# A gated mix of two attentions: the maximum of two key tiles as b + relu(a - b), with the key differences formed once, early

## The chip, the cores and the metric

The kernel runs on one core of one Trainium2 chip. A core has five engines with instruction queues of their own: TensorE (PE, matrix products; PEld is its weight load), VectorE (DVE), ScalarE (ACT), GpSimd (POOL) and SyncE (SP, which issues transfers). Products land in PSUM, eight banks of 128 partitions by 512 fp32 numbers; everything else lies in SBUF. The metric is the device time of one execution in microseconds (us); the median of three runs of the kernel before is 1503.92 us (1503.39 to 1504.63).

## The reference

```
x = A_x                                            # 1 x 2048 x 512
g = sigmoid((x * gate_w).sum(-1))
# branch A: 32 heads of 16, each query sees 8 keys at distances 0, 2, ... 14
qkv = x @ wqkv;  logits = q . k[idx] * 16**-0.5;  attn = softmax(logits)
a = (attn . v[idx]) @ wo_a
# branch B: 32 query heads of 16, one key head and one value head for all of them
q = x @ wq;  k = x @ wk;  v = x @ wv
scores = einsum("bhqd,bkd->bhqk", q, k) * 16**-0.5
b = (softmax(scores) . v) @ wo_b
out = g * a + (1 - g) * b
```

Branch B is the large part: 32 heads x 2048 queries x 2048 keys. Its weights are drawn eight times larger than those of branch A, so the scores are large and each row's maximum must be taken off before the exponential.

## The kernel before, in words

**Units and query buffers.** Branch B is cut into 32 units of four heads by 512 queries. The queries of a unit lie in a buffer `qst` (128 partitions by 2 by 512): two heads in partitions 0 to 63, two in 64 to 127, the fp32 numbers split in parts so that the fast product type keeps their digits. There are nine buffers (`NB`); unit u uses buffer u % 9. `stack(u)` fills one by four transfers on SP's queue from a DRAM scratch tensor `qd`. The keys `kst` lie in SBUF once, in the same split form, in both partition halves.

**Two passes over the scores.** The first pass needs only the maximum over all keys of each query. A unit has 64 *maximum tiles*: 128 queries by 512 keys, one product of 62 partitions each (`max_mm`). The result is reduced along the keys into `mx`. Three ways are used: a *pair* of tiles in a bank pair `pm` (`m2`), reduced by one DVE instruction (L334); a *single* tile in the bank `ps` (`m1`) or `po`, reduced by one DVE instruction (L346); and, in part of the kernel, two key tiles at once by *differences*. When a unit's 64 tiles are done, `shift_a` to `shift_d` write the negated maxima, split in two, into two spare partitions of each half of the unit's query buffer, by eight small transfers.

The second pass goes by *steps*: a step is one unit and one block of 128 keys, 16 steps per unit, 512 in all. In a step PE makes the scores again, now keys by queries and with the maximum taken off by the two extra partitions (L452, two products into each of two bank pairs `pe0`, `pe1`); ACT takes the exponential of each bank pair (L454); PE multiplies the exponentials with the values into `po` (L463, `weighted`). In between, the step takes up maximum tiles of later units: mostly one pair, and a single where `singles` allows one. `singles` spreads what is left over the steps that are left, so it decides how many steps have a single.

**The maximum by differences, before the change.** For two key tiles a and b the kernel forms, once, the half sums and half differences of the *keys*: `half_keys` multiplies `kst` by a selection matrix `sel` with entries 0.5 and -0.5 (L362), `half_parts` splits the results into `kcd`. Because a score is linear in its key, a product with the half difference gives (a - b)/2 and one with the half sum gives (a + b)/2. `fill_diff` makes the first in bank `pd0` or `pd1` (L384) and ACT writes its absolute value to SBUF (L394, `dd`). `fill_sum` makes the second in `ps` or `po` (L384), and one DVE instruction adds the two and takes the maximum (L404): (a + b)/2 + |a - b|/2 = max(a, b). So two maximum tiles cost two products, one ACT and one DVE instruction.

**The stages.** *Start*: loads, keys, the first two query blocks (L187, L824). *Query part*: the other 14 query projections, "lumps" of 12 products per array half (L1001, into four banks `pf`). *Branch A part*: 64 lumps that project branch A's queries, keys and values (L1001 too, 384 or 402 columns). *Steps*: the 512 steps, with three *output phases* among them (`out_phase`, L707) that project finished blocks. POOL computes the attention of branch A beside all this. In the query part and the branch A part, the two 64-partition halves of the array run as two streams, and maximum tiles are put between the products of the lumps. In the query part before, these are pairs and singles; `half_keys` and the differences begin with the branch A part, since `kcd`, `dd` and the two banks `pd` take memory that the query part uses for raw weights and for `pm`.

**What sets the order.** The schedule is manual: a planner in the kernel's Python keeps one clock for PE, ACT and DVE (`clk`), a time at which each bank comes free (`free`) and when a buffer is filled (`stacked`), and writes instructions engine by engine in that order when the program is built. On the chip nothing is reordered; an engine whose operand isn't ready waits. Three of the planner's rules matter here. `fillable` allows a maximum tile only for a unit whose query buffer is filled. `singles` is described above. And where a unit must soon begin its steps and its maxima aren't done (`short > 0 and steps < 2`), `pause` puts maximum tiles in a row, into `pe0`, `pe1` and `pm`, and no exponential goes on beside them.

Of the kernel before, what the change touches and what calls it, by code (L numbers as in the profile page):

```python
# [13 lines left out]
P = 128  # L14
# [34 lines left out]
def gated_mix_kernel(ctx, tc, xt, wa, wk, wq, wo_a, wo_b, out):  # L49
# [16 lines left out]
    qst = [cp.tile([P, 2, 512], F32R, name=f"qst{k}") for k in range(NB)]  # L66

# [31 lines left out]
    wqr = p0.tile([P, C, C, P], F32, name="wqr")  # L99
# [14 lines left out]
    def load_wq(cc):  # L114
        nc.scalar.dma_start(wqr[:, cc], wq[:, cc])

    def split_wq(cc):
        cs = slice(cc * P, (cc + 1) * P)
        split(wqh[:, :, cs], wql[:, :, cs], wqr[:, cc])
# [56 lines left out]
    for x in range(2):  # L176
        to = sel[:, x].rearrange("p (b h z) -> p b h z", b=2, h=2)
        nc.vector.tensor_scalar(to[:, :, 0].rearrange("p b (d s) -> p b d s", s=2), whole_k.unsqueeze(3).to_broadcast([P, 2, DH, 2]), 0.5 - x, 0.0, op0=ALU.mult, op1=ALU.add)
        nc.vector.tensor_scalar(to[:, :, 1].rearrange("p b (s d) -> p b s d", s=2), whole_k.unsqueeze(2).to_broadcast([P, 2, 2, DH]), 0.5 - x, 0.0, op0=ALU.mult, op1=ALU.add)
# [90 lines left out]

    def stack(u):
        qb, hg = divmod(u, NHG)
        for b in range(2):
# [3 lines left out]
            dst = qst[u % NB].rearrange("p c n -> p (c n)").bitcast(F32)  # L277
# [10 lines left out]
    free = {"m2": 0.0, "m1": 0.0, "e0": 0.0, "e1": 0.0, "po": 0.0}  # L288
    tasks, shifted, pm = [], set(), []
# [20 lines left out]
    def max_mm(dst, v, pr, t, kc, odd):  # L310
        b = 64 * odd
        nc.tensor.matmul(dst, qst[v % NB][b:b + 62, pr, t * P:(t + 1) * P], kst[b:b + 62, kc * 512:(kc + 1) * 512], start=True, stop=True)  # L312
# [4 lines left out]
    def filled(v, n):  # L317
        left[v] -= n
        if not left[v]:
# [7 lines left out]
            tasks.append((after("dve", 0, 0.66) + (2.0 if kcd and not pe else 0.1), shift_a, (v, mt)))  # L327
# [24 lines left out]
    kcd, dd, formed, ended = [], [], set(), set()  # L352
    pend, todo, ready_d, read_d = [[], []], [[], []], [0.0, 0.0], [0.0, 0.0]

    wanted = []

    def half_keys(g):

        clk["pe"] = max(clk["pe"], free["d0"], free["d1"])
        for x in range(2):  # L360
            for y in range(2):
                nc.tensor.matmul(ds[x], sel[:, x * y], kst[:, (2 * g + y) * 512:(2 * g + y + 1) * 512], start=(y == 0), stop=(y == 1))  # L362
        clk["pe"] += 1.2
        up = ups[0]
        free["d0"] = free["d1"] = clk["pe"] + 4.0
        tasks.append((clk["pe"] + 1.0, half_parts, (g, up)))

    def half_parts(g, up):
        for x in range(2):
            got = nc.scalar.activation(kcd[0][:, g, x], ds[x], AF.Identity, scale=mk[:, 0:1])  # L370
            at = after("act", clk["pe"], 0.65)
            mark(got, at, up)
        for x in range(2):
            parts = kcd[0][:, g, x]
            nc.vector.scalar_tensor_tensor(parts, ds[x], mk[:, 1:2], parts.bitcast(F32), op0=ALU.mult, op1=ALU.add)
            free[f"d{x}"] = after("dve", at + 0.1, 0.7) + 0.1
        formed.add(g)
# [4 lines left out]
    def half_mm(dst, v, pr, t, kc, x, odd):  # L382
        b = 64 * odd
        nc.tensor.matmul(dst, qst[v % NB][b:b + 62, pr, t * P:(t + 1) * P], kcd[0][b:b + 62, kc // 2, x, :], start=True, stop=True)  # L384

    def fill_diff(b):
# [6 lines left out]
        half_mm(ds[b], v, pr, t, kc, 1, b)  # L393
# [874 lines left out]
```

## Time and profile before

| what | value |
|---|---|
| median of three runs | 1503.92 us |
| the profiled execution | 1504.23 us, of which 1502.4 us span |
| granted clock of PE over the span | 0.998 |
| PE, PEld, DVE, ACT, POOL busy | 99%, 48%, 82%, 81%, 63% |
| 0 to 27 us | start |
| 27 to 78 us | query part |
| 78 to 274 us | branch A part |
| 274 to 1479 us | the 512 steps and three output phases |
| 1479 to 1502 us | the last rows of the output |

Times in the profile count from the span's start. A "x8" in a row is the number of instructions merged in it; what stands in brackets is how long the engine had been idle before, and what ended that. PE's busy share is high all through, but an instruction's time there runs from its start to its modelled end, and neighbours overlap: the distance between starts tells more than the busy share. The profiled execution has 1.8 us outside the span.

### The profile page before, as it was taken

The page shows a single profiled execution, that of the slowest core. Times are in us where ns is not written, and L with a number is a line of the kernel's source. Part 1 is how long each engine was busy: PE and PEld are TensorE (multiplying, and loading weights), DVE is VectorE, ACT ScalarE, POOL GpSimd, SP SyncE. Part 2 cuts the span into 40 slices and gives each one's busy share as a digit, 9 for nine tenths or more (in the row PEclk, how much of TensorE's full clock was granted, in tenths as well). Part 3 has the DMA queues.
Part 4 walks back from the last instruction along what each step waited for, and adds up shares of the span by engine and source line. Part 5 has one row for each costly group of instructions (what it writes and reads, how often), then busy time and mean ns, then how long its engine had stood idle before and what let it go on. Part 6 is the DMA issues. An engine that isn't in the chain of part 4 may idle for free.

```text
span 1502.4 us, 28913 instructions
## 1 busy us (share of the span) xinstructions
PE 1483.1 (99%) x10947; PEld 726.8 (48%) x10947; DVE 1234.6 (82%) x1777; ACT 1219.0 (81%) x1527; POOL 948.3 (63%) x1671
## 2 busy tenths in 40 slices
PE   8999999999999999999999999999999999999998
PEld 5899999433333333333333463333335533733335
DVE  6977888788888888888888888888888888888821
ACT  4357988799999999999999759999996688399884
POOL 7423988888888988888888988889812211410100
PEclk9999999999999999999999999999999999999999
DMA  6744242121221120120211112112000000000000
GB/s 219 197 125 141 83 153 94 62 77 41 62 73 41 48 77 23 65 76 12 76 41 51 59 40 70 41 40 70 13 12 8 22 2 2 30 2 1 1 2 29
DMA packets 43964, 85.63 MB, mean 57 GB/s; under 512 B 9568, under 2 KB 26016, under 8 KB 39728
## 3 DMA queue, kind: packets, MB, share of 16 engines
q1 hardware_dynamic: 36128, 43.99, 9.7%
q0 software_dynamic: 6688, 37.96, 7.6%
q8 instruction: 86, 1.41, 0.4%
q10 hardware_dynamic: 1008, 1.84, 0.4%
q14 instruction: 54, 0.44, 0.1%
HBM read 57.97 MB, written 25.25 MB: 55 GB/s over the span
## 4 chain that ended last, share of the span: by engine, by line
PE 95%; DVE 2%; ACT 1%; DMA 1%; issue 0%; POOL 0%; SPq 0%; ACTq 0%; DVEq 0%; POOLq 0%
PE po L463 33%; PE pe L452 26%; PE pf L1001 11%; PE pm L312 9%; PE ps L312 5%; PE pe L707 4%; PE pd L384 2%; DVE mx L334 1%; PE po L384 1%; PE ps L384 1%; PE pe L1199 1%; PE pf L187 1%; DMA xraw<-xt 1%; ACT pexp L454 0%; PE po L312 0%
## 5 line engine op out<-in xcount | busy, mean ns | idle before, releaser
L454 ACT ACTIVATE pexp<-pe 128x1024 f32<-128x1024 f32 x1024 | 992.4, 1023 | 103.4 <-PE pe L452 99.0
L334 DVE TENSOR_REDUCE mx<-pm 128x2 f32<-128x1024 f32 x537 | 655.7, 1221 | 149.9 <-PE pm L312 142.0
L452 PE MATMUL pe<-qst,kst 64*128 64x512 f32 x2048 | 573.5, 456 | 2.9 <-DVE mx L334 1.8
L463 PE MATMUL po<-pexp,vst 128*32 128x512 f32 x4096 | 547.0, 606 | 0.6 <-DVE tt L477 0.4
L452 PEld LDWEIGHTS pe<-qst,kst 64*128 64x128 f32 x2048 | 235.3, 184 | 441.9 <-ACT pexp L454 434.2
L346 DVE TENSOR_REDUCE mx<-ps 128x1 f32<-128x512 f32 x536 | 364.7, 680 | 5.3 <-PE ps L312 3.0
L312 PE MATMUL pm<-kst,qst 62*128 62x512 f32 x1083 | 230.8, 406 | 2.5 <-DVE mx L334 2.0
L312 PE MATMUL ps<-kst,qst 62*128 62x512 f32 x536 | 226.1, 422 | 0.6 <-DVE mx L346 0.6
L525 POOL TENSOR_TENSOR pr<-aext 128x256 f32<-128x256 f32 x256 | 182.3, 740 | 4.9 <-PE pf L1001 4.7
L585 POOL TENSOR_TENSOR oa<-oa,av 128x256 f32<-128x256 f32 x224 | 164.4, 734 | 15.8
L463 PEld LDWEIGHTS po<-pexp,vst 128*32 128x32 f32 x4096 | 80.6, 108 | 181.5 <-issue 169.4
L582 POOL TENSOR_TENSOR av<-aext,lg 128x256 f32<-128x256 f32 x224 | 139.6, 623 | 13.5
L489 POOL TENSOR_TENSOR rl<-rl,gate_t 128x16 f32<-128x16 f32 x31 | 6.9, 221 | 213.0 <-DVE rl L483 212.9
L312 PEld LDWEIGHTS ps<-kst,qst 62*128 62x128 f32 x536 | 98.5, 184 | 84.4 <-DVE mx L346 79.6
L394 ACT ACTIVATE dd<-pd 128x512 f32<-128x512 f32 x186 | 109.8, 601 | 26.0 <-DVE mx L404 15.0
L1001 PE MATMUL pf<-wah,xh 64*128 64x384 f32 (+1 forms) x496 | 124.7, 338 | 0.0
L1001 PE MATMUL pf<-wah,xl 64*128 64x384 f32 (+1 forms) x496 | 122.4, 338 | 0.0
L1001 PE MATMUL pf<-wal,xh 64*128 64x384 f32 (+1 forms) x496 | 121.3, 337 | 0.0
L312 PEld LDWEIGHTS pm<-kst,qst 62*128 62x128 f32 x1083 | 106.2, 187 | 18.3 <-DVE mx L334 11.4
L531 POOL TENSOR_TENSOR tr<-pr 128x512 f32<-128x512 f32 x64 | 81.7, 1277 | 4.2
L531 POOL TENSOR_TENSOR tr<-tr 128x256 f32<-128x256 f32 (+1 forms) x128 | 72.5, 566 | 9.0
L404 DVE CUSTOM_DVE_ANT_0 dd<-po,dd 128x512 f32<-128x512 f32 x93 | 64.2, 690 | 16.4 <-PE po L384 10.6
(198 smaller groups left out, 1688.6 us busy)
## 6 DMA issues: line engine op xcount, KB each, us to landing
aext<-ad POOLq DMA_DIRECT2D x32, 1056.0 KB, 5.4
ad<-stage SPq DMA_DIRECT2D x32, 384.0 KB
qst<-qd SPq DMA_DIRECT2D x64, 128.0 KB
xraw<-xt SPq DMA_DIRECT2D x16, 256.0 KB
qd<-qhi SPq DMA_DIRECT2D x16, 256.0 KB
qd<-qlo SPq DMA_DIRECT2D x16, 256.0 KB
qst<-qd SPq DMA_DIRECT2D x64, 64.0 KB
qst<-ml SPq DMA_DIRECT2D x224, 2.0 KB
```

The source lines that it names most:

```text
L312: nc.tensor.matmul(dst, qst[v % NB][b:b + 62, pr, t * P:(t + 1) * P], kst[b:b + 62, kc * 512:(kc + 1) * 512], start=True, stop=True)
L334: got = nc.vector.tensor_reduce(m[:, :, pr, t, kc], dst, AX.X, ALU.max)
L346: got = nc.vector.tensor_reduce(m[:, odd, pr, t, kc:kc + 1], dst, AX.X, ALU.max)
L394: got = nc.scalar.activation(dd[0][:, b], ds[b], AF.Abs)
L452: nc.tensor.matmul(bank[:, odd, :], kst[b:b + 64, kt * P:(kt + 1) * P], qst[u % NB][b:b + 64, pr, :], start=True, stop=True)
L454: got = nc.scalar.activation(e, bank, AF.Exp, scale=SCALE)
L463: nc.tensor.matmul(po[32 * i:32 * i + 32, :], vst[:, kt, :], pexp[s, i // 2][:, i % 2, :], start=(kt == 0), stop=(kt == NJ - 1))
L525: nc.gpsimd.tensor_mul(pr[:, k], q, e[:, o:o + NH, AC:2 * AC])
L531: nc.gpsimd.tensor_add(nx, cur[:, :, 0:n], cur[:, :, n:2 * n])
L582: nc.gpsimd.tensor_mul(av, e[:, o:o + NH, 2 * AC:].rearrange("p j (h d) -> p j h d", d=DH), lg[:, w].unsqueeze(3).to_broadcast([P, NH, AG, ...
L585: nc.gpsimd.tensor_add(ao, ao, av)
L1001: inst = nc.tensor.matmul(home(x)[0][:, :n], l[h], r[h], start=(i == 0 and b == 0), stop=(i == 3 * C - 1 and b == 1))
```

## The change

**The maximum.** For two key tiles a and b, max(a, b) = b + relu(a - b). The key differences a - b are still formed by a product with `sel`, now with entries 1 and -1; b is the key tile itself, as it lies in `kst`. So `fill_diff` multiplies with `kd` and ACT writes relu in place of the absolute value; `fill_sum` multiplies with `kst` by `max_mm`. The half sums aren't formed: `half_keys` is one call of four products in place of two calls of eight in all, `half_parts` splits two results in place of four.

**Memory and time.** `kd` and `dd` take the SBUF memory of the raw query weights (four blocks of `wq`, loaded and split in the start), which are from the constant pool now. The two banks `pd0`, `pd1` exist from the start, in place of the bank pair `pm`, which comes only with the steps. So `half_keys` runs at the beginning of the query part, and differences are used there already. The first pair before the query part is gone, and the maximum tiles are taken unit by unit from the start.

**Query buffers.** The buffers of the output phases (`own`, `turned`) are no longer tiles of their own: they lie in query buffers 7 and 8, which after units 7 and 8 hold no queries. Units from 9 on go round through seven buffers (`place`). `stack` is therefore called two units later from the sixteenth unit on, and the last rows use other buffers.

```diff
+    wq01 = cp.tile([P, 2, 512], F32, name="wq01", tag="kd", bufs=1)
+    dd = cp.tile([P, 2, 512], F32, name="dd")
...
-    pp2 = tc.alloc_tile_pool(name="pairs", bufs=1, space=PSUM)
-    m2 = pp2.tile([P, 2, 512], F32, name="pm")
-    ds = []
+    pp2, m2 = None, None
+    pools = [tc.alloc_tile_pool(name="parts", bufs=1, space=PSUM)]
+    ds = [pools[0].tile([P, 512], F32, name=f"pd{k}") for k in range(2)]
...
+    def place(v):
+        return v if v < NB else (v - NB) % (NB - 2)
...
-    slots = [(v, pr, t, kc) for kc in range(2) for v in range(2) for pr in range(2) for t in range(4)]
-    slots += [(v, pr, t, kc) for v in range(2) for pr in range(2) for t in range(4) for kc in range(2, 4)]
-    slots += [(v, pr, t, kc) for v in range(2, NU) for pr in range(2) for t in range(4) for kc in range(4)]
+    slots = [(v, pr, t, kc) for v in range(NU) for pr in range(2) for t in range(4) for kc in range(4)]
...
-    def half_keys(g):
+    def half_keys():
         clk["pe"] = max(clk["pe"], free["d0"], free["d1"])
-        for x in range(2):
-            for y in range(2):
-                nc.tensor.matmul(ds[x], sel[:, x * y], kst[:, (2 * g + y) * 512:(2 * g + y + 1) * 512], start=(y == 0), stop=(y == 1))
+        for y in range(2):
+            for g in range(2):
+                nc.tensor.matmul(ds[g], sel[:, y], kst[:, (2 * g + y) * 512:(2 * g + y + 1) * 512], start=(y == 0), stop=(y == 1))
...
-        half_mm(ds[b], v, pr, t, kc, 1, b)
-        got = nc.scalar.activation(dd[0][:, b], ds[b], AF.Abs)
+        diff_mm(ds[b], v, pr, t, kc, b)
+        got = nc.scalar.activation(dd[:, b], ds[b], AF.Relu)
...
-        half_mm(dst, v, pr, t, kc, 0, b)
+        max_mm(dst, v, pr, t, kc + 1, b)
...
-        hi, lo = turned[j, 1] = [pe[0].tile([P, C, P], F32R, name=f"own{x}", bufs=1) for x in range(2)]
+        hi, lo = turned[j, 1] = [qst[NB - 2][:, x].rearrange("p (c q) -> p c q", c=C) for x in range(2)]
...
-        if len(stacked) < NU and s >= 16 * (len(stacked) - NB + 1):
+        if len(stacked) < NU and s >= 16 * (len(stacked) - NB + 1 + 2 * (len(stacked) >= 2 * NB - 2)):
```

Since the planner fills gaps by rule, the change moves maximum tiles through the whole program. Three places show it, each in PE's row of instructions (PE is the engine that the others wait for there). The first is in the query part, while its second and third lumps run (`pf`); `ps`, `po`, `pm` and `pd` are banks of maximum tiles. PE before:

```order
L1001 MATMUL pf_95<-xh,wql 128x512
L312 MATMUL ps<-kst,qst_77 128x512
L1001 MATMUL pf_95<-xh,wqh 128x512
L1001 MATMUL pf_95<-xl,wqh 128x512
L1001 MATMUL pf_96<-xl,wqh 128x512
L312 MATMUL po<-kst,qst_77 128x512
L1001 MATMUL pf_96<-xh,wql 128x512
L1001 MATMUL pf_96<-xh,wqh 128x512
```

PE after, at the first differences:

```order
L386 MATMUL pd_93<-kd,qst_76 128x512
L1002 MATMUL pf_99<-xl,wqh 128x512
L1002 MATMUL pf_99<-xh,wql 128x512
L1002 MATMUL pf_98<-xh,wqh 128x512
L1002 MATMUL pf_99<-xh,wqh 128x512
L1002 MATMUL pf_98<-xl,wqh 128x512
L315 MATMUL ps<-kst,qst_76 128x512
L1002 MATMUL pf_98<-xh,wql 128x512
```

A product into `ps` that was a single is now the b of a pair of tiles whose difference went to `pd`. In the query part the maximum tiles go from 73 to 99.

The second place is the forming of the key differences. PE before, in the branch A part (the first of two such pieces):

```order
L1001 MATMUL pf_96<-wal,xh 128x402
L362 MATMUL pd_1004<-kst,sel 128x512 x2
L362 MATMUL pd_1005<-kst,sel 128x512 x2
L312 MATMUL ps<-kst,qst_76 128x512
L312 MATMUL po<-kst,qst_76 128x512
```

PE after, in the first lump of the query part, among singles:

```order
L315 MATMUL po<-kst,qst_76 128x512
L1002 MATMUL pf_97<-xh,wqh 128x512
L1002 MATMUL pf_97<-xl,wqh 128x512
L365 MATMUL pd_92<-kst,sel 128x512
L365 MATMUL pd_93<-kst,sel 128x512
L365 MATMUL pd_92<-kst,sel 128x512
L365 MATMUL pd_93<-kst,sel 128x512
L1002 MATMUL pf_97<-xh,wql 128x512
```

Eight such products became four, and they stand at the beginning of the query part.

The third place is the end of the maximum tiles, 24 steps before the end. `pe` with `qst` as the first operand is a step's scores, `pe` with `kst` first is a maximum tile that took an exponential's bank. PE before:

```order
L463 MATMUL po<-pexp,vst 32x512 x4
L312 MATMUL pe_3947<-kst,qst_80 128x512
L312 MATMUL pm<-kst,qst_80 128x512 x2
L312 MATMUL pe_3948<-kst,qst_80 128x512 x2
L312 MATMUL pe_3947<-kst,qst_80 128x512 x2
L312 MATMUL pm<-kst,qst_80 128x512 x2
L452 MATMUL pe_3947<-qst_79,kst 128x512 x2
L312 MATMUL ps<-kst,qst_80 128x512
L452 MATMUL pe_3948<-qst_79,kst 128x512 x2
L463 MATMUL po<-pexp,vst 32x512 x4
```

PE after, at the last maximum tiles and the first rows of the output's end (`ident`), which before follow a little behind the piece shown:

```order
L454 MATMUL pe_4050<-qst_76,kst 128x512 x2
L315 MATMUL pm<-kst,qst_77 128x512 x2
L454 MATMUL pe_4051<-qst_76,kst 128x512 x2
L465 MATMUL po<-pexp,vst 32x512 x4
L454 MATMUL pe_4050<-qst_76,kst 128x512 x2
L746 MATMUL pm<-ident,oa 128x64 x4
L746 MATMUL pm<-ident,oa_4111 128x64 x4
L454 MATMUL pe_4051<-qst_76,kst 128x512 x2
```

The planner no longer comes to the `pause` there. Counted over the built program, by stage (maximum tiles in PE's row; a step is *full* if it holds a single, *light* if not; "after" and "before" are the kernels):

| | before | after |
|---|---|---|
| maximum tiles ahead of the query part | 4 | 2 |
| maximum tiles in the query part | 73 | 99 |
| maximum tiles in the branch A part, up to the first `weighted` | 408 | 429 |
| products with `sel` | 8 | 4 |
| full steps | 441 | 421 |
| light steps | 65 | 87 |
| steps of the pause | 2 | 0 |
| maximum tiles in the three output phases | 149 | 145 |

More of the change, by code (lines that the diff above doesn't have):

```diff
@@ L98, in gated_mix_kernel @@
     wkr = p0.tile([P, C, P], F32, name="wkr")
-    wqr = p0.tile([P, C, C, P], F32, name="wqr")
+    wqr = [t[:, k].rearrange("p (c q) -> p c q", c=C) for t in (wq01, dd) for k in range(2)]
     waraw, wah, wal = {}, {}, {}
@@ L311, in max_mm @@
         b = 64 * odd
-        nc.tensor.matmul(dst, qst[v % NB][b:b + 62, pr, t * P:(t + 1) * P], kst[b:b + 62, kc * 512:(kc + 1) * 512], start=True, stop=True)
+        nc.tensor.matmul(dst, qst[place(v)][b:b + 62, pr, t * P:(t + 1) * P], kst[b:b + 62, kc * 512:(kc + 1) * 512], start=True, stop=True)
     def to_go():
@@ L371, in half_parts @@
             at = after("act", clk["pe"], 0.65)
             mark(got, at, up)
[L373 to L377, printed above, removed]
+        for g in range(2):
+            nc.vector.scalar_tensor_tensor(kd[0][:, g], ds[g], mk[:, 1:2], kd[0][:, g].bitcast(F32), op0=ALU.mult, op1=ALU.add)
+            free[f"d{g}"] = after("dve", at + 0.1, 0.7) + 0.1
+            formed.add(g)
@@ L451, in exp_pair @@
             b = 64 * odd
[L452 removed]
+            nc.tensor.matmul(bank[:, odd, :], kst[b:b + 64, kt * P:(kt + 1) * P], qst[place(u)][b:b + 64, pr, :], start=True, stop=True)
         e = px.tile([P, 2, 512], F32, name="pexp", bufs=6)
@@ L732, in last_parts @@
     def last_parts(c):
-        hi, lo = store["b", c] = [qst[(NU - 9 + c) % NB][:, x, :] for x in range(2)]
+        hi, lo = store["b", c] = [qst[place((NU - 7, NU - 6, NU - 4)[c])][:, x, :] for x in range(2)]
         nc.gpsimd.tensor_copy(hi, ob[NQB - 1][:, c, :])
@@ L1027, in done_mm @@
             branch_a()
-            pm.append(tc.alloc_tile_pool(name="maxima", bufs=1, side="right"))
-            dd.append(pm[0].tile([P, 2, 512], F32, name="dd", bufs=1))
-            kcd.append(pm[0].tile([P, 2, 2, 512], F32R, name="kcd", bufs=1))
-            pp2.release()
-            pools.append(tc.alloc_tile_pool(name="parts", bufs=1, space=PSUM))
-            ds.extend(pools[0].tile([P, 512], F32, name=f"pd{k}") for k in range(2))
-            free["d0"] = free["d1"] = free.pop("m2")
-            wanted.extend([0, 1])
         if x == last and i == 9:
```

56 lines of the change are left out of this document (27 added, 29 removed).

## The prediction

> **What bounds the kernel now.** I read the page's busy shares and its chain first, then stretches of each stage, then single steps, then the end of the steps.
>
> ```profile
> PE 1483.1 (99%) x10947; PEld 726.8 (48%) x10947; DVE 1234.6 (82%) x1777; ACT 1219.0 (81%) x1527; POOL 948.3 (63%) x1671
> PE 95%; DVE 2%; ACT 1%; DMA 1%; issue 0%; POOL 0%; SPq 0%; ACTq 0%; DVEq 0%; POOLq 0%
> ```
>
> PE is busy nearly always and the chain that ended last is PE's own, so what counts is what PE does, and where it stands still inside that busy time. The stretches (columns: PE, PEld, DVE, ACT, POOL busy with their numbers of instructions, PE clock, DMA share, GB/s):
>
> ```profile
> 27.30:35.00 7.70, 7.10 (x45) 5.46 (x44) 7.39 (x11) 2.76 (x6) 7.70 (x7) 1.00 0.52 156
> 35.00:80.00 45.00, 45.00 (x381) 40.24 (x380) 44.06 (x67) 15.71 (x31) 22.05 (x21) 1.00 0.67 189
> 80.00:100.00 20.00, 20.00 (x180) 18.11 (x178) 15.62 (x28) 7.29 (x21) 3.70 (x5) 1.00 0.49 145
> 140.00:260.00 120.00, 120.00 (x1261) 118.79 (x1259) 99.67 (x303) 104.50 (x216) 106.11 (x205) 1.00 0.38 121
> 400.00:500.00 100.00, 99.92 (x697) 35.03 (x694) 87.49 (x108) 91.84 (x102) 84.99 (x165) 1.00 0.17 53
> ```
>
> From 35 us PE streams without a break: 381 products in 45.00 us, nearly all of 512 columns on one array half, make **0.118 us for a product**, the price of a maximum tile in the query part. DVE, which must reduce each of these tiles, is busy 44.06 of 45 us there: it, not PE, keeps more tiles out of the query part. Now single steps, by PE's timeline:
>
> ```profile
> 480.03 1.06 PE L463 MATMUL po<-pexp,vst 128*32 128x512 f32 x8
> 481.60 0.41 PE L312 MATMUL ps<-kst,qst 62*128 62x512 f32 x1
> 482.17 1.06 PE L463 MATMUL po<-pexp,vst 128*32 128x512 f32 x8
> 484.16 1.06 PE L463 MATMUL po<-pexp,vst 128*32 128x512 f32 x8
> ...
> 485.73 0.39 PE L312 MATMUL ps<-kst,qst 62*128 62x512 f32 x1
> 486.28 1.06 PE L463 MATMUL po<-pexp,vst 128*32 128x512 f32 x8
> ```
>
> Between the starts of two `weighted` blocks lies one step. With a single in `ps` it takes 2.14 and 2.12 us, without one 1.99 us. Over many steps (instructions by group from 400 to 800 us, and the exponentials alone from 1436.6 to 1478.6 us, where no maximum tile is left):
>
> ```profile
> L454 ACT ACTIVATE pexp<-pe 128x1024 f32<-128x1024 f32 x373 | 361.8, 1023 | 33.0 <-PE pe L452 31.0 <-PE pm L312 0.3
> L346 DVE TENSOR_REDUCE mx<-ps 128x1 f32<-128x512 f32 x169 | 114.8, 679 | 0.0
> 1436.60:1478.60 42.00, 40.10 (x42) 1.00 0.01 1
> ```
>
> Two exponentials are a step: 400 us hold 186.5 steps, 2.145 us each, 169 of them with a single; the last 42.00 us hold 21, 2.00 us each, and there ACT is the bound (40.10 of 42.00). Pairs fit in the light step of 1.99 us, so a single costs (2.145 - 2.00) x 186.5 / 169 = **0.16 us**, a full step 2.16 and a light one 2.00. Last, the end of the maximum tiles, with the clock:
>
> ```profile
> 1423.29 1.06 PE L463 MATMUL po<-pexp,vst 128*32 128x512 f32 x8
> ...
> 1428.96 0.79 PE L452 MATMUL pe<-qst,kst 64*128 64x512 f32 x2 [1.76 <-DVE mx L334]
> ...
> 1430.54 1.93 PE L463 MATMUL po<-pexp,vst 128*32 128x512 f32 x8
> ...
> 1433.97 1.70 PE L463 MATMUL po<-pexp,vst 128*32 128x512 f32 x8
> ...
> 1436.56 0.64 PE L463 MATMUL po<-pexp,vst 128*32 128x512 f32 x4
> ```
>
> ```profile
> 1423.30:1430.50 7.20, 4.49 (x23) 1.83 (x22) 6.90 (x8) 2.00 (x3) 0.00 (x0) 0.86 0.01 2
> 1430.50:1434.00 3.50, 3.50 (x18) 1.05 (x17) 0.75 (x2) 1.99 (x3) 0.00 (x0) 0.50 0.00 0
> ```
>
> The planner's pause: three steps take 13.27 us. PE waits for DVE's reductions, and is then granted half its clock: `weighted` takes 1.93 and 1.70 us in place of 1.06.
>
> **The change part by part.**
>
> *Maximum tiles that move forward.* Up to the first `weighted` there are 2 + 99 + 429 = 530 in place of 4 + 73 + 408 = 485: 45 more, x 0.118 = **+5.3 us** of PE work ahead of the steps. They fit because a difference costs DVE one instruction for two tiles:
>
> ```profile
> L394 ACT ACTIVATE dd<-pd 128x512 f32<-128x512 f32 x186 | 109.8, 601 | 26.0 <-DVE mx L404 15.0 <-PE pd L384 4.9 <-PE po L384 1.8
> L404 DVE CUSTOM_DVE_ANT_0 dd<-po,dd 128x512 f32<-128x512 f32 x93 | 64.2, 690 | 16.4 <-PE po L384 10.6 <-ACT dd L394 3.4 <-ACT gate_t L266 0.4
> ```
>
> DVE pays 690 ns for two tiles in place of 679 for one; ACT gets 45 times 601 ns in the query part, 27 us on top of its 15.71 in 45. Relu for the absolute value and `kst` for the half sums I cost at nothing: same shapes, same engines.
>
> *Forming the keys.* Eight full-array products go, each worth two half-array ones: 8 x 0.236 = **-1.9 us**. The four new ones (0.94 us) fall at about 29 us, where PE makes 45 products (5.3 us) in 7.70 us and stands idle for the rest behind DVE's first reductions: I cost them at 0, at +0.9 if that cover is gone. Around the old place PE wasn't dense either:
>
> ```profile
> L1001 PE MATMUL pf<-wah,xh 64*128 64x402 f32 x48 | 12.7, 348 | 0.0
> L1001 PE MATMUL pf<-wal,xh 64*128 64x402 f32 x48 | 12.3, 344 | 0.0
> L1001 PE MATMUL pf<-wah,xl 64*128 64x402 f32 x46 | 11.9, 343 | 0.0
> L362 PE MATMUL pd<-kst,sel 128*128 128x512 f32 x8 | 2.4, 421 | 0.0
> ```
>
> Of the 180 products from 80 to 100 us these are 142 at 0.118 x 402/512 = 0.093 (13.2 us) and 8 at 0.236 (1.9); the other 30 take 3.5. That is 18.6 of 20: 1.4 us idle, while the planner holds tiles back until the key parts are ready. After, differences run on through: **-1.0** (0 to -1.4).
>
> *Waits between ACT, DVE and PE in the query part.* The trace has no differences beside query lumps. Nearest rows: 140 to 260 us, differences beside lumps of branch A, PE streaming with its weight loads at 118.79 of 120 us, so 0; and 80 to 100 us, 1.4 lost in 20, over 45 us +3.2. I take **+1.0**, nearer the first since ACT and DVE carry about the same load there.
>
> *The steps.* 20 full steps fewer (-43.2 us), 22 light ones more (+44.0), and the two steps of the pause go together with the slow step behind them (13.27 - 2.00 = 11.27): **-10.5 us**. Of this the pause is 7.1 to 7.3 us over ordinary steps, the singles 3.2. If a single costs nothing, -7.3 remains; with the single light step's 1.99 beside 2.16, a single costs 0.17 and -10.7 comes out. Output phases: four tiles fewer at 0.118, **-0.5**.
>
> *Query buffers.* `stack` for unit 9 stands on SP's queue where it stood; what is new is that its first maximum tile comes two steps later.
>
> ```profile
> 305.46 0.61 SPq L278 DMA_DIRECT2D qst<-qd  x1
> ...
> 307.41 0.58 SPq L279 DMA_DIRECT2D qst<-qd  x1
> ```
>
> The four issues took 2.5 us; the landing isn't shown. Two steps are 4 us, so the wait is between 0 and some 3 us, once; I take 0, since later fills stand ten steps and more ahead of their use. The output phases wait for the same engines in their new buffers: 0.
>
> *Sum.* Ahead of the steps 5.3 - 1.9 - 1.0 + 1.0 = +3.4 (bounds +2.0 to +7.5); steps -11.0 (-7.8 to -11.2). Together **-7.6 us** from the profiled execution's 1504.23: 1496.6. The median is 0.3 lower than that execution, so I predict 1496.3.
>
> **The rivals.**
>
> *Singles are free in the steps.* PE's products overlap, and PEld is busy only 35.03 of 100 us in the steps; then removing tiles there would free nothing, only the pause's 7.3 and the 0.5 would be saved, and the time would be 1504.2 + 3.4 - 7.8 = 1499.8, 1499.5 by the median. The Trainium skill (Perfetto Trace Analysis, Identifying the Most-Contended Engine) says just this of such a profile: matmul busy time doesn't tell headroom, weight-load busy time does; by it the front, at 118.79 of 120, has none and the steps have much. Against it stand the steps themselves, 2.14 and 2.12 us with a single and 1.99 without. Chance 0.17.
>
> *The query part chokes (the other side).* Relu, the copies of finished lumps and the sums stand in three in-order queues; if ACT (15.71 + 27 of 45 us) comes late, PE waits in both halves and the lumps with it. To end slower by 3 us, the front must lose 10.6 us more than I gave it, a quarter of the query part; the time would be some 1508. Against it: at 140 to 260 us ACT is busy 104.50 of 120 and PE streams. Chance 0.08; a choke half that size, ending near 1502, 0.08.
>
> *The wait moves to the last unit.* Without the pause the last unit's maxima end later in steps, and its shift transfers could come too late for its first step.
>
> ```profile
> 1434.70 0.21 DVE L324 STREAM_TRANSPOSE mt<-ms 128x32 f32<-128x32 f32 x1
> ...
> 1439.07 2.57 SPq L440 DMA_DIRECT2D qst<-ml  x4
> ```
>
> That gives back about the pause's 7 us: 1503.4. Against it: from the transpose to the last issue are 7 us, and the order leaves nine light steps, 18 us. Chance 0.05. That the change doesn't do what it says is excluded by the built order for the counts.
>
> **How the numbers follow.** My forecast, -4.5 to -11 us: 0.62; then 0.17, 0.16 and 0.05 as above. A measurement here tells 0.2%, 3 us, from no change. Faster: 0.62 + 0.16 of the first rival = 0.78. Within 0.2%: 0.05 of the last, 0.08 of the half choke = 0.13. Slower 0.09. The range 1491.5 to 1502.0 takes the low bounds (1504.2 - 11.2 + 2.0 = 1495.0, and 3.5 us for idle time of PE that the change may fill and no row tells) and reaches over the free singles to the half choke; about 0.2 is left out.
>
> **What would show it.** Right: no product `pe<-kst` and no granted clock of 0.5 near the end; light steps near 2.00 and full ones near 2.16, some 20 more and fewer; the first `weighted` about 3 us later than 274.7; a dense PE from 80 to 100 us. Wrong: light steps as long as full ones; ACT or DVE named ahead of PE between 30 and 80 us; a hole ahead of the first tiles of unit 9 or the last unit.

## The result and the profile after

The changed kernel takes 1499.72 us (median of 22 executions, 1498.35 to 1504.74); the kernel before, on the same chip, takes 1503.80 us (22 executions, 1503.33 to 1506.51). The ratio is 0.9981 with a 95% interval of 0.9973 to 0.9989. The time lies in the predicted range, but 1496.3 us, a gain of 7.6 us, was predicted; 4.1 us came by the medians and 2.9 by the ratio.

The 22 executions do not scatter, they fall into two groups: twelve between 1498.35 and 1499.80 us with a mean granted clock of PE of 1.000, and ten between 1502.56 and 1504.74 us with 0.996 or 0.997. (The expectations quoted below say nine; it is ten.) The profiled execution, 1504.74 us with a span of 1503.0 us, is of the second group. A second profile of the same kernel (e10 below) fell into the first: 1499.31 us, span 1497.5 us.

First the stretches that the prediction read, in the second group's profile (columns: PE, PEld, DVE, ACT, POOL busy with their numbers of instructions, PE clock, DMA share, GB/s), and the start of the first `weighted` by PE's timeline:

```profile
27.30:35.00 7.70, 6.63 (x22) 3.83 (x21) 3.61 (x6) 5.12 (x10) 7.70 (x7) 0.79 0.48 151
35.00:80.00 45.00, 44.95 (x345) 38.96 (x346) 31.09 (x84) 31.36 (x62) 18.03 (x20) 0.92 0.54 146
80.00:100.00 20.00, 20.00 (x190) 18.74 (x189) 14.27 (x42) 16.84 (x34) 8.95 (x9) 1.00 0.66 194
140.00:260.00 120.00, 118.93 (x1228) 115.58 (x1228) 97.92 (x298) 102.47 (x214) 98.19 (x192) 1.00 0.37 117
```

```profile
285.02 1.06 PE L465 MATMUL po<-pexp,vst 128*32 128x512 f32 x8
```

Then the same of the first group's profile:

```profile
27.30:35.00 7.70, 6.63 (x31) 4.17 (x33) 5.41 (x9) 4.46 (x9) 7.70 (x8) 1.00 0.57 169
35.00:80.00 45.00, 44.95 (x380) 40.65 (x381) 33.02 (x92) 35.88 (x70) 21.03 (x22) 1.00 0.58 159
80.00:100.00 20.00, 20.00 (x202) 19.62 (x200) 14.14 (x44) 16.67 (x39) 6.35 (x9) 1.00 0.62 186
140.00:260.00 120.00, 118.99 (x1234) 116.18 (x1235) 98.76 (x299) 103.43 (x213) 102.76 (x200) 1.00 0.40 126
```

```profile
279.34 1.06 PE L465 MATMUL po<-pexp,vst 128*32 128x512 f32 x8
```

PE is "busy" for the same 44.95 us from 35 to 80 us in both, but makes 345 products in the one and 380 in the other (before: 381). The clock column tells the difference: 0.79 and 0.92 against 1.00. The last `weighted` starts at 1478.64 us before, at 1479.36 in the second group's profile and at 1473.86 in the first's, so front and steps come apart like this:

| | before | forecast | first group | second group |
|---|---|---|---|---|
| first `weighted` starts at (us) | 274.68 | +3.4 | 279.34 (+4.7) | 285.02 (+10.3) |
| from there to the last one (us) | 1203.96 | -11.0 | 1194.52 (-9.4) | 1194.34 (-9.6) |
| execution (us) | 1504.23 | -7.6 | 1499.31 (-4.9) | 1504.74 (+0.5) |

The steps did nearly what was forecast, in both groups alike. At the place of the pause PE's timeline of the first group's profile now has

```profile
1423.75 1.06 PE L465 MATMUL po<-pexp,vst 128*32 128x512 f32 x8
1425.86 1.07 PE L465 MATMUL po<-pexp,vst 128*32 128x512 f32 x8
1427.81 1.06 PE L465 MATMUL po<-pexp,vst 128*32 128x512 f32 x8
1429.87 1.07 PE L465 MATMUL po<-pexp,vst 128*32 128x512 f32 x8
```

ordinary steps of 1.95 to 2.11 us, and `weighted` stays at 1.06 or 1.07. What failed is the front, and it failed in two ways. The second group's timeline of PE at 28 us shows the first:

```profile
28.82 0.39 PE L1002 MATMUL pf<-xh,wqh 64*128 64x512 f32 x1
30.27 0.50 PE L315 MATMUL ps<-kst,qst 62*128 62x512 f32 x1 [1.07 <-DVE mx L349]
...
31.76 2.06 PE L365 MATMUL pd<-kst,sel 128*128 128x512 f32 x4
33.76 0.79 PE L1002 MATMUL pf<-xh,wql 64*128 64x512 f32 x1
```

PE stands for 1.07 us behind DVE's reduction, the four products that form the differences then take 2.06 us (1.22 in the first group's profile), and lump products 0.79 in place of 0.39. The same stretches by windows, with the two that hold the clock's fall and its return:

```profile
27.40:31.70 4.30, 3.23 (x14) 1.63 (x12) 2.83 (x5) 3.76 (x8) 4.30 (x4) 1.00 0.53 169
31.70:42.00 10.30, 10.30 (x37) 8.20 (x38) 5.21 (x9) 1.26 (x2) 5.11 (x5) 0.51 0.13 40
31.75:32.00 0.25, 0.25 (x2) 0.24 (x2) 0.25 (x1) 0.00 (x0) 0.25 (x2) 0.61 0.01 0
42.00:42.25 0.25, 0.25 (x5) 0.25 (x3) 0.25 (x1) 0.00 (x0) 0.00 (x0) 0.91 0.00 0
```

The trace records only 0.5 and 1.0 as values of the clock, so a mean of 0.61 in the window from 31.75 puts the fall at 31.80 us, and 0.91 in that from 42.00 the return at 42.05: 10.24 us at half clock, 5.1 us of PE's work lost. In the same 10.30 us the kernel before made 83 products, this execution 37.

### The profile page after: what moved, and what is told of

Its sections match the earlier page's. It is cut to its first block, busy times and chain, and to the rows that moved or that the text cites. A ratio compares the mean times of both kernels' runs of the same rounds, so it can differ in the third digit from the quotient of the medians.

```text
span 1503.0 us, 29096 instructions
## 1 busy us (share of the span) xinstructions
PE 1481.7 (99%) x10945; PEld 730.0 (49%) x10945; DVE 1198.1 (80%) x1789; ACT 1251.3 (83%) x1591; POOL 944.5 (63%) x1667
## 4 chain that ended last, share of the span: by engine, by line
PE 93%; DVE 3%; ACT 1%; issue 1%; DMA 1%; DVEq 0%; ACTq 0%
PE po L465 32%; PE pe L454 25%; PE pf L1002 11%; PE pm L315 8%; PE ps L315 5%; PE pe L709 5%; PE pd L386 2%; DVE mx L337 1%; PE po L315 1%; PE pf L189 1%; DVE mx L349 1%; DVE tt L479 1%; PE pe L1192 1%; DMA ad<-stage 0%; ACT pexp L456 0%
## 5 line engine op out<-in xcount | busy, mean ns | idle before, releaser
L337 DVE TENSOR_REDUCE mx<-pm 128x2 f32<-128x1024 f32 x525 | 641.0, 1221 | 165.7 <-PE pm L315 158.0
L349 DVE TENSOR_REDUCE mx<-ps 128x1 f32<-128x512 f32 x476 | 323.9, 681 | 8.3 <-PE ps L315 7.3
L315 PE MATMUL ps<-kst,qst 62*128 62x512 f32 x602 | 252.4, 419 | 1.1 <-DVE mx L349 1.1
L315 PE MATMUL pm<-kst,qst 62*128 62x512 f32 x1054 | 222.7, 404 | 0.8 <-DVE mx L337 0.6
L396 ACT ACTIVATE dd<-pd 128x512 f32<-128x512 f32 x252 | 147.6, 603 | 30.7 <-DVE mx L406 16.5
L315 PEld LDWEIGHTS ps<-kst,qst 62*128 62x128 f32 x602 | 111.2, 185 | 78.9 <-DVE mx L349 74.4
L1002 PE MATMUL pf<-wah,xh 64*128 64x384 f32 (+1 forms) x496 | 117.2, 338 | 0.0
L406 DVE CUSTOM_DVE_ANT_0 dd<-po,dd 128x512 f32<-128x512 f32 x126 | 87.0, 691 | 31.8 <-PE po L315 17.8
L406 DVE CUSTOM_DVE_ANT_0 dd<-ps,dd 128x512 f32<-128x512 f32 x126 | 87.0, 690 | 19.4 <-PE ps L315 5.6
L386 PE MATMUL pd<-kd,qst 62*128 62x512 f32 x252 | 100.8, 405 | 1.1 <-ACT dd L396 1.0
```

Of the source, the lines that this page charges most:

```text
L315: nc.tensor.matmul(dst, qst[place(v)][b:b + 62, pr, t * P:(t + 1) * P], kst[b:b + 62, kc * 512:(kc + 1) * 512], start=True, stop=True)
L337: got = nc.vector.tensor_reduce(m[:, :, pr, t, kc], dst, AX.X, ALU.max)
L349: got = nc.vector.tensor_reduce(m[:, odd, pr, t, kc:kc + 1], dst, AX.X, ALU.max)
L396: got = nc.scalar.activation(dd[:, b], ds[b], AF.Relu)
L406: got = nc.vector.tensor_tensor_reduce(dd[:, b], dst, dd[:, b], 1.0, -FMAX, ALU.add, ALU.max, m[:, b, pr, t, kc:kc + 1])
L1002: inst = nc.tensor.matmul(home(x)[0][:, :n], l[h], r[h], start=(i == 0 and b == 0), stop=(i == 3 * C - 1 and b == 1))
```

## Theories

After the two profiles there were four. **Clock, by the hole** (theory 1 in the expectations): PE's thin work between 27 and 32 us makes the clock fall, in some executions. **Clock, by the burst** (theory 2): the four full-array products at 31.76 us, where the fall is, cause it. **Late data** (theory 3): the group has nothing to do with what PE does. **Queue** (theory A): apart from the clock, something in branch A's part holds PE up, since even the first group reaches the steps 1.3 us later than forecast.

The experiments ran in three jobs on three chips, each beside the kernel before: it took 1504.37 us beside e1 to e4, 1503.08 beside e5 to e7 and 1504.53 beside e8 to e10. Across jobs the ratios to it are compared, not the times.

## Experiments on the clock

**e1_dummy8: more work in the hole.**

```diff
     fill_one(po, "po")
+    for k in range(8):
+        nc.tensor.matmul(ds[k % 2], sel[:, 0], kst[:, 0:512], start=True, stop=True)
     split_x(3, nc.gpsimd)
```

> The changed kernel with eight extra full-array products of `kst` by `sel` (results thrown away) on PE right after the first two maximum tiles, at about 28 us. The changed kernel's executions fall into two groups, near 1499.2 us with a mean granted clock of 1.000 and near 1503.9 us with 0.997, and its profiled one (second group) shows the clock at 0.50 from 31.7 to 42 us. Theory 1 (PE's thin work between 27.4 and 32 us, some 3 us of idle time there, makes the clock fall): the extra products (8 x 0.236 = 1.9 us) fill the hole, every execution has clock 1.000, one group between 1499 and 1501 us, although work was added. Theory 2 (the burst of four full-array products at 31.76 us, all 128 rows at once, makes it fall): three times the burst, so the second group has at least as many executions as now (9 of 22), near 1504 to 1506 us. Theory 3 (late data or queue waits, nothing to do with what PE does): the shares stay as they are, both groups up to 1.9 us later.

Measured: 1502.71 us (11 executions, 1500.48 to 1504.27), clock 0.999 or 1.000 in ten and 0.998 in one, none at 0.997 or below. Its windows:

```profile
27.40:31.70 4.30, 4.30 (x20) 3.02 (x18) 2.69 (x5) 3.17 (x7) 4.30 (x5) 1.00 0.56 168
31.70:42.00 10.30, 10.30 (x70) 8.17 (x70) 7.83 (x14) 3.50 (x7) 5.88 (x5) 1.00 0.23 64
```

Three bursts in place of one, and no fall in the profile: the burst theory is out. (The one execution at 0.998 leaves room for a shorter fall somewhere; it has no profile.) The time is 1.7 us above the expected range, though; its profile shows a wait of ACT of 3.25 us near 200 us, to which the queue experiments come back.

**e2_gap: a longer hole.**

```diff
     fill_one(m1, "m1")
+    for _ in range(3):
+        nc.vector.tensor_reduce(unit_tile(0)[:, 0, 0, 0, 0:1], m1, AX.X, ALU.max)
     fill_one(po, "po")
```

> The changed kernel with DVE's first reduction of the bank `ps` done four times instead of once at about 28.5 us (3 x 0.69 = 2.1 us), so that the third maximum tile and all products behind it on PE wait 2.1 us longer. Theory 1: more idle time on PE ahead of 32 us, so the clock falls in nearly all executions: one group near 1505 to 1507 us, clock 0.996. Theories 2 and 3: the share of the executions with a low clock stays near 9 of 22, and both groups come 0 to 2 us later than 1499.2 and 1503.9 us.

Measured: 1507.63 us (8 executions, 1505.01 to 1509.42), clock 0.995 to 0.997 in every one. In its windows PE is busy 1.36 of 4.30 us ahead of the fall, and the fall lasts longer:

```profile
27.40:31.70 4.30, 1.36 (x7) 0.79 (x6) 3.17 (x5) 3.31 (x7) 4.30 (x5) 0.97 0.56 181
31.25:31.50 0.25, 0.00 (x0) 0.00 (x0) 0.24 (x1) 0.00 (x0) 0.25 (x2) 0.94 0.65 213
45.00:45.25 0.25, 0.25 (x4) 0.25 (x3) 0.25 (x2) 0.00 (x0) 0.00 (x0) 0.76 0.00 0
```

From 31.47 to 45.12 us, 13.65 us. That all executions now fall, and the change of the shares with it, is what the hole theory says and the late-data theory doesn't.

**e3_form36: the burst moved away, the hole kept.** The planner is told that the two difference banks are free later; the products that form the differences then came at 40.98 us.

```diff
-    free = {"m1": 0.0, "e0": 0.0, "e1": 0.0, "po": 0.0, "d0": 29.0, "d1": 29.0}
+    free = {"m1": 0.0, "e0": 0.0, "e1": 0.0, "po": 0.0, "d0": 36.0, "d1": 36.0}
```

> The changed kernel with the forming of the key differences put off from about 31 to about 36 us; ahead of it maximum tiles are taken as in the changed kernel, so PE still waits for DVE at 29 us, but the four full-array products no longer stand at 31.8 us. Nine tiles fewer lie ahead of the first `weighted` (521 for 530). Theory 1: two groups as before, near 1499 and 1504 us, the second with a clock of 0.5 for some 10 us from about 32 us. Theory 2: the fall moves to about 36 us with the burst, or, between dense products, is gone: then one group near 1499 us.

Measured: 1506.89 us (11 executions, 1503.66 to 1508.57), clock 0.995 to 0.999, no two clean groups. In its profile the clock falls at 30.10 us, ahead of the burst, and returns at 36.92, after 6.83 us:

```profile
30.00:30.25 0.25, 0.25 (x2) 0.25 (x2) 0.25 (x1) 0.25 (x1) 0.25 (x1) 0.69 0.98 246
36.75:37.00 0.25, 0.25 (x4) 0.15 (x4) 0.00 (x0) 0.00 (x0) 0.00 (x0) 0.66 0.00 0
```

The burst is out for a second time. That all executions are some 4 us later than expected isn't the clock at 30 us alone: this kernel waits longer in branch A's part (ACT 6.1 us for `ad<-stage`), and the clock falls a second time at 269 us.

**e4_late_singles: no hole, the burst kept.** The planner takes DVE as busy until 30 us, so that it puts nine lump products, not four, ahead of the third maximum tile.

```diff
-    clk.update(pe=26.5, act=26.5, dve=26.5)
+    clk.update(pe=26.5, act=26.5, dve=30.0)
```

> The changed kernel with one number of the planner changed: it takes DVE as busy up to 30 us instead of 26.5, so that nine lump products instead of four come ahead of the third maximum tile and PE needn't wait for DVE's first reductions; the four full-array products of the forming stay at about 31 us. Ten tiles fewer lie ahead of the first `weighted` (520 for 530). Theory 1: no hole, clock 1.000 in every execution, one group, 1497.5 to 1499.5 us, faster than both kernels by the median. Theory 2: the burst is still there, so the two groups stay, near 1499 and 1504 us. Theory 3: two groups with unchanged shares.

Measured: 1498.14 us (5 executions, 1497.14 to 1500.29), clock 0.999 or 1.000; ratio to before 0.9963 (0.9951 to 0.9976). One group:

```profile
27.40:31.70 4.30, 4.30 (x21) 3.00 (x19) 1.95 (x3) 4.15 (x9) 4.30 (x5) 1.00 0.56 168
31.70:42.00 10.30, 10.30 (x83) 9.57 (x83) 8.26 (x17) 4.63 (x10) 5.78 (x5) 1.00 0.40 111
```

83 products in the second window, as many as before the change. Five executions are few, but e5 and e7 have the same front, and their ten show no clock below 0.999 either. With e1 and e2 this settles the cause: more work in the hole, thrown-away products or lump products, takes the fall away, less brings it always.

The first group's own profile has the hole as well, 3.23 of 4.30 us busy (x15), without a fall. The kept traces show what decides there. Each records when the clock first rose to 1.0 in the start: at 11.33 us in the second group's profile, and the fall at 31.81 comes 20.48 us later, six times 3.413. In e2 and e8 it comes 23.89 us after the rise, seven times 3.413. So the clock changes only on a grid of 3.413 us, which begins at another point in each execution. Below stand the last piece of the grid ahead of the fall, in the second group's profile and in e8's (the changed kernel with another edit, below), and the two pieces around the hole in the first group's, where the clock rose at 8.53:

```profile
28.39:31.81 3.42, 2.35 (x11) 1.17 (x9) 2.94 (x5) 2.77 (x6) 3.42 (x3) 1.00 0.39 117
28.24:31.66 3.42, 2.35 (x12) 1.26 (x9) 2.75 (x5) 2.95 (x6) 3.42 (x3) 1.00 0.59 189
25.60:29.01 3.41, 2.95 (x10) 1.23 (x8) 1.52 (x4) 3.41 (x8) 2.97 (x3) 1.00 0.71 209
29.01:32.43 3.42, 2.81 (x12) 1.63 (x13) 2.44 (x4) 1.79 (x4) 3.42 (x4) 1.00 0.42 121
```

Where the hole lies in one piece, 2.35 us busy, the clock falls at its end; where a boundary cuts the hole, neither piece is that thin, and it doesn't. That rests on one undisturbed profile of the changed kernel; the kernel before has 2.82 us busy in its piece from 29.02 us, and no fall. PE's busy time alone isn't the measure: in e1 the piece from 202.23 us has 1.78 us busy, with 18 products, and no fall.

## Experiments on the queue

In the second group's profile ACT's and SP's timelines and SP's waits show why PE is idle near 200 us. ACT copies finished lumps of branch A into one of two `stage` buffers; a buffer is free again when its store `ad<-stage` (L255, on SP's queue) has landed. The shift transfers `qst<-ml` (L442), eight for each unit whose maximum is done, are on the same queue.

```profile
205.31 0.49 ACT L246 ACTIVATE stage<-pf 128x384 f32<-128x384 f32 x1 [1.68 <-DMA ad<-stage]
```

```profile
190.07 0.36 SPq L255 DMA_DIRECT2D ad<-stage  x1
197.28 1.29 SPq L442 DMA_DIRECT2D qst<-ml  x2
198.67 0.36 SPq L255 DMA_DIRECT2D ad<-stage  x1
199.09 4.57 SPq L442 DMA_DIRECT2D qst<-ml  x6
```

```profile
SPq L442 <- POOL ml L431: 6.8, 1, 6.8
```

```profile
200.00:206.00 6.00, 5.33 (x56) 4.94 (x53) 3.86 (x12) 3.86 (x8) 5.37 (x10) 1.00 0.90 298
```

The copy that the store at 198.67 carries was done at 195.2 us. At the head of SP's queue, ahead of it, stood the first shift transfer, waiting 6.8 us in all for POOL; two shift issues later the store went out, 3.5 us late. ACT waits for it until 205.31, the relus behind it wait, and PE loses 0.67 of 6 us.

The late issue is only half of that wait. The chain of work shows how long the store was under way:

```profile
198.67 6.54 DMA ad<-stage
```

It landed 6.5 us after its issue, where the stores issued at 190.07 and 203.75 took 2.6. POOL issues two loads, at 197.20 and 198.71, and the DMA engines are 0.90 busy in the window above: the late store met other transfers. Another store of this profile, at 253.69, is 3.5 us late too, lands in 2.6 us, and nothing waits for it.

**e5_shifts_spread: the shift transfers spread, on top of e4.**

```diff
-            tasks.append((clk["pe"] + (1.2 if pe else 0.8) * k, shift_d, (v, ml, k)))
+            tasks.append((clk["pe"] + (1.2 * k if pe else 6.0 + 1.8 * k), shift_d, (v, ml, k)))
```

> The kernel e4_late_singles with the eight small shift transfers of each unit that ends ahead of the steps put 6 us later and 1.8 us apart instead of 0.8, so that the stores of branch A stand between them on SP's queue instead of behind all eight. Theory A (the shift transfers hold up the stores, ACT's next copy into `stage` waits for the store, and PE for ACT): ACT's waits for the transfer `ad<-stage` (1.6 us in the profile of e4, 1.7 in that of the changed kernel, none before the change) are gone, and the time falls by 0.5 to 2 us, to 1496 to 1497.6. Rival (ACT's wait lies beside other waits): the wait is gone or not, the time stays at 1498.1 within 0.4.

Measured: 1496.46 us (5 executions, 1496.19 to 1497.01); ratio to the kernel before, 1503.08 us there, 0.9954 (0.9941 to 0.9966). That is 1.7 us below e4 by the times and 1.3 by the ratios, whose intervals overlap; e8 and e10, in one job, tell more. No wait of ACT is put down to `ad<-stage` in its profile any more. This is the best version of the study, faster than both kernels.

**e8_spread_alone: the same edit on the changed kernel.**

> The changed kernel with only the shift transfers ahead of the steps put 6 us later and 1.8 us apart (as in e5), the planner's number left at 26.5 us: same steps and tiles as the changed kernel. Clock theory and queue theory are independent: the hole at 27 to 32 us stays, so two groups stay, some 9 of 22 executions with a clock near 0.997; ACT's waits for `ad<-stage` are gone, so both groups come about 1.7 us earlier than the changed kernel's, near 1497.5 and 1502.2 us. If the shifts matter only together with the planner's number: 1499.2 and 1503.9 as now.

Measured: 1498.04, 1498.13 and 1498.18 us with a clock of 0.999 or 1.000, 1502.57 and 1503.40 with 0.996. The changed kernel itself, on the same chip (next run), has medians of 1499.89 and 1504.17: both groups stay, each 1.2 to 1.8 us earlier, and no execution of e8 is as late as the earliest of the same group there. Its SP queue and the same 6 us of PE:

```profile
189.67 5.49 SPq L255 DMA_DIRECT2D ad<-stage  x2
196.86 1.28 SPq L442 DMA_DIRECT2D qst<-ml  x2
```

```profile
200.00:206.00 6.00, 6.00 (x67) 6.00 (x65) 4.94 (x15) 4.99 (x10) 5.45 (x9) 1.00 0.52 193
```

The second of the two stores, issued at 194.80 us, now goes out ahead of the shifts and of POOL's loads (196.77 and 198.28), lands in 2.6 us, and PE is dense. The edit took the late issue and the meeting with the loads away together; which of the two alone would do wasn't tried.

**e9_before_spread: the same edit on the kernel before.**

> The kernel before with the same edit of the shift transfers; steps, tiles and pause as before. The profile of before shows no wait of ACT for `ad<-stage`, so by the queue theory nothing is to be had: within 0.7 us of the kernel before. If the edit helps any kernel of this build: 1.5 us faster, as from e4 to e5, and then it doesn't explain what the change lost.

Measured: 1504.42 us (11 executions) against 1504.53 of the kernel before, ratio 0.9999 (0.9990 to 1.0008). Nothing was to be had where ACT doesn't wait. Stores stand behind shifts in the kernel before too: one goes out at 214.74 us, 3.9 us late behind eight of them, but it lands in 2.6 us, 2.0 us ahead of the copy that needs its buffer. By the trace the shift transfers ahead of the steps are 56 before, seven units, and 64 after, eight units; the change moved them against the stores and POOL's loads.

**e10_changed_again: the changed kernel once more.**

> The changed kernel itself, for a second profile. If it falls into the group with a clock of 1.000: span near 1497.5, the first `weighted` near 279.7 us instead of 285.0 (5.3 us less in the stretch from 31 to 43 us, nothing else different), and ACT's wait of 1 to 3 us for `ad<-stage` near 200 us is there too.

Measured: ten executions, three at 1499.31 to 1500.52 us (clock 0.999 to 1.000), seven at 1504.07 to 1505.15 (0.996 to 0.997); median 1504.12, ratio 0.9990 (0.9980 to 1.0000). So the share of the groups isn't fixed, 12 of 22 in one job and 3 of 10 in this one, and the kernel's median hangs on it. The profile is the first group's above. Span and first `weighted` came as expected; the wait near 200 us is there too, 1.62 us ahead of the copy at 199.63. This profile puts it down to PE, but the store issued at 193.04, 3.5 us late, landed at 199.52, after 6.5 us again, and the copy follows 0.1 us behind it.

## Experiments on the steps

**e6_late_forming: e4 with the differences formed late** (the two numbers of e3, at 75.0), which leaves the memory, the banks and the buffers as the change has them and takes back the early use.

> The kernel e4_late_singles with the forming of the key differences put off from about 31 to about 75 us: 478 maximum tiles instead of 522 ahead of the first `weighted` (before: 485), 19 full steps more and 15 light ones fewer, and the planner's pause is back near the end of the steps. By the prediction's prices: front 44 x 0.118 = -5.2, singles 19 x 0.16 = +3.0, pause +7.2, together +5.0, 1503.1 us. If singles are free in the steps: -5.2 + 7.2 = +2.0, 1500.1. If the pause costs nothing: -5.2 + 3.0, 1495.9.

Measured: 1506.54 us (11 executions, 1505.44 to 1507.57), clock 0.995 to 0.997; ratio to before 1.0021 (1.0012 to 1.0030). The pause is back, larger than before, in PE's timeline:

```profile
1421.05 1.06 PE L465 MATMUL po<-pexp,vst 128*32 128x512 f32 x8
1433.70 1.94 PE L465 MATMUL po<-pexp,vst 128*32 128x512 f32 x8
1437.14 1.93 PE L465 MATMUL po<-pexp,vst 128*32 128x512 f32 x8
1440.15 1.06 PE L465 MATMUL po<-pexp,vst 128*32 128x512 f32 x8
```

Three steps take 19.10 us, 12.9 more than three ordinary ones of 2.07, where 7.2 was put in: 5.7 us more, which is more than the whole 3.4 us by which the expectation was missed. The clock is a large part of it: by windows as above it is at half from 1425.76 to 1439.42 us here, and for 6.83 us at the pause of the kernel before, which makes 3.4 us of PE's work. Both rivals, at 1500.1 and 1495.9, are out. The gain of the change hangs on the early differences, and comes through the pause.

**e7_singles_twice: the price of a single in a step.**

```diff
-        max_mm(dst, v, pr, t, kc, odd)
+        for _ in range(2 if pe and 300 <= len(slots) < 450 else 1):
+            max_mm(dst, v, pr, t, kc, odd)
```

> The kernel e4_late_singles with the product of about 100 singles in the steps done twice into the same bank, so that PE does 100 half-array products more, DVE and ACT nothing more. By the prediction (a single costs 0.16 us in a step, PE is the bound): +16 us, 1514; if only the 0.118 of its product counts, +12, 1510. Rival (singles are free in the steps, PE has room there): 1498 to 1499 us.

Measured: 1514.17 us (5 executions), 16.0 above e4 by the times and 17 by the ratios. Two steps with a doubled single and one without any, by PE's timeline:

```profile
850.86 1.07 PE L466 MATMUL po<-pexp,vst 128*32 128x512 f32 x8
852.43 0.63 PE L315 MATMUL ps<-kst,qst 62*128 62x512 f32 x2
853.23 1.07 PE L466 MATMUL po<-pexp,vst 128*32 128x512 f32 x8
854.80 0.62 PE L315 MATMUL ps<-kst,qst 62*128 62x512 f32 x2
855.59 1.06 PE L466 MATMUL po<-pexp,vst 128*32 128x512 f32 x8
857.47 1.06 PE L466 MATMUL po<-pexp,vst 128*32 128x512 f32 x8
```

2.37 and 2.36 us with two products, 1.88 without; full steps with one take 2.169 on the mean. PE has no room in these steps.

## Why the prediction was wrong, and where it was right

**The step that failed** is the part of the front that took PE's idle time as free: "The four new ones (0.94 us) fall at about 29 us, where PE makes 45 products (5.3 us) in 7.70 us and stands idle for the rest behind DVE's first reductions: I cost them at 0, at +0.9 if that cover is gone". The cover itself was misread: 45 products at 0.118 us make 5.3 of 7.70 us, but PE's row there says 7.10 of 7.70 busy. In the first lump only one array half has lump products, and their starts lie 0.23 us apart; the idle time was 0.6 us. And the prediction asked how much work fits into the idle time, not what the idle time does to the work behind it. The kernel before had 3.70 of 4.30 us busy with 19 products there. The change took the early pair out, so that four lump products, not eight, stand ahead of the third maximum tile, and 3.23 us with 14 or 15 products are left. In ten of 22 executions the clock is then lower; in the profiled one it stays at half for 10.24 us, 5.1 us that the sum did not have. The prediction had quoted the same event at 1430 us, as a cost of the pause, and asked only whether it goes away there. No rival named it; the "half choke", near 1502 us, comes closest to the second group's time, by another mechanism. That the median lies in the range is luck in part: it hangs on how many executions fall, and in e10 it was 1504.12.

**The front without the fall.** The 1824 lump products into `pf` are the same in both kernels, so their starts show where the first group's profile falls behind the kernel before. Some of that is further products ahead of them, priced at 0.118 us for one on an array half; the rest is waiting, lost or saved:

| lump product | before (us) | first group | later by | further products | rest |
|---|---|---|---|---|---|
| 61st | 39.02 | 41.50 | 2.5 | 1.1 | +1.4 |
| 301st | 74.30 | 79.16 | 4.9 | 3.9 | +1.0 |
| 481st | 98.87 | 102.12 | 3.3 | 4.2 | -1.0 |
| 1261st | 195.81 | 198.60 | 2.8 | 4.6 | -1.8 |
| 1381st | 210.57 | 215.14 | 4.6 | 4.5 | +0.1 |

At the 61st the further products are the four that form the differences (0.9) and one maximum tile: the early forming and its hole cost some 2.3 us in the undisturbed group too, where 0 was put in, 0.9 at most. *The waits*, +1.0 us between ACT, DVE and PE in the query part, were the wrong waits: none was to be seen there in the undisturbed profile (380 products from 35 to 80 us against 381). The dense stretch, -1.0 from 80 to 100 us, was better than forecast, -2.0 (202 products against 180). The late store near 200 us then took 1.9 back, which the sum didn't have; the prediction followed SP's queue for the query buffers alone. So +4.7 comes near the forecast +3.4 with errors both ways.

**The steps**: -9.4 and -9.6 in place of -11.0. Between the starts of `weighted` in the trace, 441 full steps became 421, both at 2.167 us on the mean, -43.2 us as forecast. But 64 light steps of 1.982 us became 87 of 2.004: with the pause (three steps, 13.27 us) gone that is +34.2, where +44.0 - 11.3 = +32.7 was forecast with 2.00 for both. The output phases gave 0.4 us for 0.5. A mis-sized term, the mechanism right.

**The rivals.** Singles are not free: 0.16 us each by the same counts (2.167 - 2.004), and a doubled one costs 0.19. The Trainium skill (Perfetto Trace Analysis, Identifying the Most-Contended Engine) would have PE's headroom judged by the arithmetic done, as a share of the peak, and by the weight loads, 35 of 100 us here; for the weight loads e7 speaks against that in these steps. The last unit had no wait: the steps after 1423 us are ordinary. The first rival's time, 1499.5 us, is nearly the measured median; its reason is refuted all the same.

**Right** were the counts, the end of the pause and its worth, and the absence of a hole at the new query buffers. Without the two accidents the total comes near the forecast: e5, with ten early tiles fewer than the change, is 6.9 us faster than the kernel before by its ratio, where 7.6 was forecast.

## What to carry to other kernels

Idle time of PE early in a kernel isn't free cover: when a change thins PE's work out for some microseconds, price the half clock that may follow, and look at the clock of each execution before averaging over two groups. When work moves, follow the queues that carry the small transfers of the moved work, not only those of the moved instructions: a store behind an issue that waits for another engine goes out late, and what that costs depends on the transfers that it then meets. Both were mended by a number of the planner each, 1.2 to 1.8 us and a whole group of executions for no work saved.

## What the runs showed of the hardware

The time at half clock came in equal pieces: 6.83 us in e3, 10.24 in the second group, 13.65 in e2, two, three and four times 3.41. The Trainium skill (TensorE: Matmul & The Clock Gate, What's actually happening) states a free-running window of 3413 ns, and the lengths agree, as does the grid found after e4. The Trainium skill's rule for kernels (same page, Why this matters for your kernels) asks only that PE have no idle gap of more than about 3 us; here the clock fell behind a gap of 1.07 us, with PE shown busy for 2.35 of the last 3.42 us, nearly all of it half-array products, so thin work can be enough. What exactly is counted stays open. The Trainium skill (same page, What's actually happening) has the clock return after one busy window or more; one wasn't enough here: PE's row shows 10.30 of 10.30 us busy at half clock, three windows of it.

A store that took 2.6 us from issue to landing took 6.5 when it met POOL's loads, with the DMA engines 0.90 busy.
